# Batch 1's folds begin four units later, w_out's first conversion step moves between P's two parts, and w_in's third transform is cut into three pieces

## The chip, the core and the metric

The kernel runs on one core of a Trainium2 chip. The metric is the time of one execution on the device in microseconds (us); lower is better. The core has TensorE (PE, matrix products; PEld is its loading of weights), VectorE (DVE), ScalarE (ACT) and GpSimd (POOL), each with its own stream of instructions that it works through in order, and SyncE (SP), which here only issues DMA transfers. POOL issues DMA transfers too, and computes between them.

## What is computed

The reference takes a two-dimensional Fourier transform of each of four batches, keeps the real part, and sends the tokens through two feed-forward blocks:

```python
X = np.fft.fft(np.fft.fft(x, axis=1), axis=2).real      # x: 4 x 3072 x 256
h = X @ w_in                                            # 256 -> 2048
g = np.maximum(0.01 * h, h) @ w_out                     # 2048 -> 256
xk = mu_k * g + (1 - mu_k) * g_prev                     # g_prev: the token before
xr = mu_r * g + (1 - mu_r) * g_prev
k = np.maximum(xk @ w_k, 0)
out = 1 / (1 + np.exp(-(xr @ w_r))) * (k * k @ w_v)
```

The weights are float64 in memory.

## The kernel before

**Shape of the work.** The transform over the 256 columns is folded into w_in (in eight pieces of 256 columns, `w_in_mm`), so that h comes out of two half-width products: P (from the even half, tiles `Ph` and `Pl`, a high and a low part) and Q (the odd half, `Qh`, `Ql`). The transform over the 3072 tokens is made of four products a batch, "Pe", "Qe", "Po" and "Qo", each with two tables (`fft_a` and `fft_b`), from a folded copy of the input, `pm`. Each product is taken in high and low parts, three matrix products for one.

**Units.** The first feed-forward block runs in 192 units: four batches b, three tiles ti of 512 token pairs, sixteen blocks u of 128 hidden columns. Inside a batch the unit has the number i = 16 ti + u. A unit (`step`) is, on PE: `mm_b` of this unit (L597, three matmuls), `mm_a` of the next (L585, three), and `outmm` of the unit two before (L608, twelve: `gh` by `uoh`, `gh` by `uol`, `gl` by `uoh`). DVE makes `g` (L674) and the next unit's `ev` (L590), then `gl` (L656); ACT makes the two leaky copies of `g` (L108) and `gh` (L105). `mm_b` needs `ev`, and `outmm` needs `gl` and the piece of w_out that belongs to it.

**Boot.** During batch 0's first tile the weights are still converted from float64, a piece every two units (`boot`). A piece of w_out goes through eight steps: head (ACT, L130), and (DVE, L134), two (DVE, L140), three (DVE, L143), tail (ACT, L148, then POOL, L149), four (ACT, L162, then POOL, L163) and five (DVE, L167, which writes `uol`). Piece q is used by `outmm` of units 2q and 2q + 1.

**Folds.** While batch b runs, batch b + 1's `pm` is made in six folds g (`fold_ops`): `first(g)` has SP load a quarter into `pm` (L210) and two quarters into a buffer `xl` (L211; two buffers in turn); `second(g)` has POOL add the other quarters by accumulating DMA (L215 to L218: the first waits for the load into `pm`, L216 for the load into `xl`, L217 for the addition of L215, and L218 for that of L217); `fin(g)` is a subtraction on DVE (L221) that reads `xl`. There is one `pm`, so that `first(0)` cannot start before the last reader of the old one, Qe's second half at i = 11. The folds' results are first read at i = 36 (Po).

**What sets the order.** Everything is written out by hand: an engine's stream is the order in which the Python code emits instructions, and engines wait for each other by semaphores. For batch 0 the folds are emitted at i = 11 (folds 0 and 1 loaded, fold 0's additions) and then from f0 = 13 to f1 = 36 by the rule `done * (f1 - f0) < 6 * (i - f0 + 1)`, which comes to `fin` at i = 13, 16, 20, 24, 28 and 32; each brings the next `second` and the `first` after that.

**Start.** Ahead of the first unit stand `first_p` and `first_q` (batch 0's Po and Qo, straight into `Ph`, `Pl` and `Q`), then the conversion of w_out's piece 0 (`head0`, `and0`, `two0`, `three0`, `tail0`), and the third piece of `w_in_mm`, half of it after the first `mm_a` and half in `boot(0)`.

Of the kernel before, what the change touches and what calls it, by code (L numbers as in the profile page):

```python
# [78 lines left out]
def fft_mlp_kernel(ctx, tc, xs, x7, x8, x87, tb, tbs, alt, ce, so, mu, w_in, w_out, w_k, w_v, w_r, out):  # L79
    nc = tc.nc  # L80
    ctx.enter_context(tc.manual_schedule())
    V, A, T, G, Q = nc.vector, nc.scalar, nc.tensor, nc.gpsimd, nc.sync
# [21 lines left out]
    def act_copy(o, i):  # L104
        A.activation(o, i, ACTF.Copy)  # L105
# [217 lines left out]
            Q.dma_start(y[0:1, :CW[par]], cd[par][b:b + 1, :CW[par]])  # L323
        classes[b, nm, par] = y

    def first_p(ps, ev):
        fft_mm(0, "Po", 1, ps, True)
        y = pqp.tile([P, CP], F32, tag="P", bufs=2, name="c0Po")
        classes[0, "P", "o"] = y
        hi = mv.tile([P, W], F32R, tag="Ph", bufs=2, name="Ph0_0")  # L330
        lo = mv.tile([P, W], F32R, tag="Pl", bufs=2, name="Pl0_0")
        act_copy(hi[:, :J], ps[:, :J])
        V.scalar_tensor_tensor(y[:, J:2 * J], ev[:, :J], 2.0, ps[:, :J], op0=ALU.mult, op1=ALU.subtract)
        V.tensor_tensor(lo[:, :J], ps[:, :J], hi[:, :J].bitcast(F32), op=ALU.subtract)
        hi_lo(hi[:, J:], lo[:, J:], y[:, J:W])
        return [hi, lo]

    def first_q(ps, ev):
        fft_mm(0, "Qo", 1, ps, True)
        y = pqp.tile([P, CP], F32, tag="Q", bufs=2, name="c0Qo")  # L340
        classes[0, "Q", "o"] = y
        act_copy(y[:, :J], ps[:, :J])
        n = W - J
        V.scalar_tensor_tensor(y[:, J:W], ev[:, :n], -2.0, ps[:, :n], op0=ALU.mult, op1=ALU.add)
        act_copy(y[0:1, :J], cs0[0:1, :J])
        act_copy(y[0:1, J:W], cs0[0:1, J:W])

        def rest():
            V.scalar_tensor_tensor(y[:, W:2 * J], ev[:, n:J], -2.0, ps[:, n:J], op0=ALU.mult, op1=ALU.add)
            act_copy(y[0:1, W:CW["o"]], cs0[0:1, W:CW["o"]])  # L350
        return rest
# [42 lines left out]
            win[q] = f64_parts(win[q], 2, 256, F32R)  # L394


    def w_in_mm(q, halves=(0, 1)):
        if q >= 8:
            return
        if halves[0] == 0:  # L400
            wps[q] = *win[q], ps_s.tile([P, 512], F32, tag="s", name=f"wps{q}")
        fv, r, ps = wps[q]
        win[q] = ps, slice(q * 256, (q + 1) * 256)
        for i in halves:
            tabl, tabr = ((cet, cer), (sot, sor))[i]
            o = ps[:, i * 256:(i + 1) * 256]
            for k in range(2):
                T.matmul(o, tabl[:, k], fv[:, k], start=(k == 0), stop=False)
            for k in range(2):
                T.matmul(o, tabr[:, k], r[:, k], start=False, stop=(k == 1))  # L410

    def w_in_split(q):
        if q >= 8:
            return
        ps, sl = win[q]
        o = ps.rearrange("p (i f) -> p i f", i=2)
        act_copy(wh2[:, :, sl], o)
        V.tensor_tensor(wl2[:, :, sl], o, wh2[:, :, sl].bitcast(F32), op=ALU.subtract)
# [122 lines left out]
    po = fft_a(0, "Po")  # L541
# [1 line left out]
    for g in range(3, 6):  # L543
        fold_odd(g, x0[g])
    w_in_parts(2)
    cur = first_p(*po)
    head0, and0, two0, three0, tail0 = wout[0][3]
    rest_q = first_q(*qo)
    head0()
    and0()  # L550
    rows.release()
    wo = tc.alloc_tile_pool(name="wo", bufs=1)
# [5 lines left out]
    def boot(u):  # L558
        q = u // 2
        if u == 0:  # L560
            w_in_mm(2, (1,))
            three0()
            tail0()
            wout[0][1]()
            w_in_load(4)
        elif u % 2 == 0:
            w_in_row(q + 1)
            w_in_mm(q + 2)
            if q < 8:
                wout[q][0]()  # L570
                wout[q][1]()
            w_in_load(q + 4)
        else:
            w_in_split(q + 2)
            wout[q][2]()
            w_in_parts(q + 3)
            w_out_load(q + 3)
# [243 lines left out]
    rest_q()  # L821
    for b in range(B):

        pe_u, qe_u, f0, f1 = (5, 10, 13, 36) if b == 0 else (1, 4, 10, 36)
        po_u, qo_u = 37, 40
        done = 0
        for ti in range(NT):
# [3 lines left out]
            for u in range(NF):  # L831
                i = ti * NF + u
                x = nx
                if u < NF - 1:
                    nx = unit(b, ti, u + 1, cur, cur_c)
                elif not last:
                    cur, cur_c = nxt, nxt_c
                    nx = unit(nb, nt, 0, cur, cur_c)
                else:
                    nx = None  # L840
                step(x, nx)
                if b == 0 and ti == 0:
                    boot(u)
                if b == 0 and i < 2:
                    next_tab()
                if b == 0 and i == 0:
                    alt2 = work.tile([2, JP], F32, tag="fv", bufs=2, name="alt2")
                    Q.dma_start(alt2, alt)
                if b == 0 and i == 1:
                    even0(0, 1)  # L850
                    even0(1, 1)
                    act_copy(altt[0:2], alt2)
                    V.tensor_tensor(c87[0:1], x87t[:, 0], x87t[:, 1], op=ALU.add)
                if b == 0 and i == 3:
                    chalf = c_a(c8s, "a", True)
                if b == 0 and i == 4:
                    c_b(c8s, "b", "e", *chalf, "yo")

                for kb, kind, k_u in ((b, "Pe", pe_u), (b, "Qe", qe_u), (b + 1, "Po", po_u), (b + 1, "Qo", qo_u)):
                    if kb == B:  # L860
                        continue
                    lag = 2
                    if i in (k_u - 1, k_u + 1):
                        fft_src(kb, kind, (i - k_u + 1) // 2)
                    if i == k_u:
                        half = fft_a(kb, kind)
                    if i == k_u + lag:
                        fft_b(kb, kind, *half)
                    if i in (k_u, k_u + lag):
                        next_tab()  # L870
                if i == qe_u + 1:
                    if b + 1 < B:
                        first, second, fin, _, load7, sum7, fold7 = fold_ops(b + 1)
                        first(0)
                        first(1)
                        load7()
                        second(0)
                if b == B - 1 and i == qe_u + 2:
                    fft.release()
                    w2_alloc()  # L880
                if b + 1 < B:
                    while f0 <= i and done < 6 and done * (f1 - f0) < 6 * (i - f0 + 1):
                        fin(done)
                        if done < 5:
                            second(done + 1)
                        if done < 4:
                            first(done + 2)
                        done += 1
                        if done == 2:
                            sum7()  # L890
                        if done == 4:
                            fold7()
                if i == 13:
                    dc_split(b)
                if 14 <= i < 18:
                    dc_mm(b, i - 14)
                if i == 18:
                    dc_load(b)
                if i == 26:
                    dc_g(b)  # L900
                if b == 0 and i == 34:
                    w2_load[0]()
                if len(w2_steps) > 5 * (len(sources) - n_early):
                    if po_u <= i < po_u + 5 or (b > 0 and i < 5):
                        w2_steps.pop(0)()
                elif b == B - 1 and i > 7 and w2_steps and i % 3:
                    w2_steps.pop(0)()
                if b == B - 1:
                    if i == 33:
                        Q.dma_start(mut, mu)  # L910
                    if i == 36:
                        V.tensor_scalar(omu, mut, -1.0, 1.0, op0=ALU.mult, op1=ALU.add)
                        loaded[0] = load_tile(0)
                    if i == 39:
                        todo = do_prep(0)
                    if i in (40, 42, 44, 46):
                        todo.pop(0)()
                if not last:
                    if u == 8:
                        nxt_c = load_c(nb, nt)  # L920
                    if u == (9 if b or ti else 12):
                        nxt = split_tile(nb, nt, "P")
                    if u == (12 if b or ti else 14):
                        nxt += split_tile(nb, nt, "Q")
# [90 lines left out]
    for ti in range(len(tiles)):  # L1015
# [3 lines left out]
        f0, f1, g0 = (0, 2, 4) if ti else (2, 5, 5)  # L1019
# [3 lines left out]
        for f in range(f0, NK):  # L1023
            ps = ps2.tile([P, 512], F32, tag="k", bufs=2, name="kps")
# [110 lines left out]
```

## Time and profile before

| | |
|---|---|
| median of 3 runs | 1501.49 us (1501.39 to 1501.73) |
| the profiled execution's own time | 1500.71 us |
| its span, first to last instruction | 1498.9 us |
| PE busy | 1475.7 us, 98% |
| DVE busy | 1025.5 us, 68% |
| ACT busy | 893.8 us, 60% |
| POOL busy | 145.4 us, 10% |
| mean granted clock of PE | 0.997 |

The profiled execution took 0.78 us less than the median, and 1.8 us of its time lie outside its span. Shares are of the span. PE's clock has two levels, 1.2 and 2.4 GHz; 1.00 stands for 2.4, and a mean between 0.5 and 1 over a stretch is a mixture in time.

### The profile page before, as it was taken

Reading aid. Unit: us, or ns where it says so; the run is one execution under the profiler, and the core shown is the slowest. Engines: PE = TensorE matmul, PEld = TensorE weight load, DVE = VectorE, ACT = ScalarE, POOL = GpSimd, SP = SyncE. Lnnn points to the kernel's source line nnn. Section 1 sums busy time; section 2 is a strip of 40 time slices with the busy share of each in tenths; the row PEclk is TensorE's granted clock in tenths of the full one; section 3 lists DMA queues with packets and bytes.
Section 4 is the critical chain, followed back from the end, with each engine's and each line's share of the span. In section 5 each row is a group of like instructions: output and inputs, shape, how many; then the busy total and the mean of one; then the engine's idle time right before and its main releaser. Section 6 shows DMA issues by size and latency. Waiting matters only on the chain.

```text
span 1498.9 us, 17784 instructions
## 1 busy us (share of the span) xinstructions
PE 1475.7 (98%) x6520; PEld 1212.7 (81%) x6520; DVE 1025.5 (68%) x1444; ACT 893.8 (60%) x1481; POOL 145.4 (10%) x154
## 2 busy tenths in 40 slices
PE   7997999999999999999999999999999999999998
PEld 4785888888888888888888887888888888888887
DVE  7885667666667666676667765776767676666675
ACT  4674556656556656666566665656555656555554
POOL 2434201122001131010010000000000000000000
PEclk9998999999999999999999999999999999999999
DMA  8755414365123554132320102221212121221200
GB/s 312 200 163 130 71 49 156 102 173 93 29 72 119 192 108 92 39 124 92 109 57 22 56 1 84 84 80 48 85 42 85 45 82 57 71 70 57 71 29 29
DMA packets 86396, 134.24 MB, mean 90 GB/s; under 512 B 29283, under 2 KB 49525, under 8 KB 82724
## 3 DMA queue, kind: packets, MB, share of 16 engines
q1 hardware_dynamic: 70916, 86.49, 17.7%
q0 software_dynamic: 15392, 46.61, 12.4%
q8 instruction: 51, 0.84, 0.2%
q14 instruction: 37, 0.30, 0.1%
HBM read 105.20 MB, written 27.88 MB: 89 GB/s over the span
## 4 chain that ended last, share of the span: by engine, by line
PE 90%; DVE 1%; DMA 1%; POOL 1%; issue 0%; ACT 0%; POOLq 0%; ACTq 0%; DVEq 0%
PE o L608 32%; PE v L975 17%; PE kps L932 17%; PE ps L597 8%; PE ps L585 8%; PE rps L983 4%; DMA pm<-in_xs 1%; PE dps L629 0%; POOL r L163 0%; POOL r L149 0%; PE f1Qe L300 0%; PE f2Qe L300 0%; DMA y<-yo 0%; PE f3Qe L300 0%; PE f3Pe L300 0%
## 5 line engine op out<-in xcount | busy, mean ns | idle before, releaser
L674 DVE SCALAR_TENSOR_TENSOR g<-ev,ps 128x512 f32<-128x512 f32 x192 | 131.7, 686 | 182.3 <-PE ps L597 182.3
L936 ACT ACTIVATE rl<-kps 128x512 f32<-128x512 f32 x190 | 113.5, 597 | 230.7 <-PE kps L932 227.3
L656 DVE TENSOR_TENSOR gl<-g,gh 128x1024 fp32r<-128x1024 f32 x192 | 236.8, 1234 | 1.6 <-ACT gh L105 1.6
L937 DVE SCALAR_TENSOR_TENSOR k<-kps,rl 128x512 f32<-128x512 f32 x190 | 131.3, 691 | 148.6 <-ACT rl L936 147.8
L105 ACT ACTIVATE gh<-g 128x1024 fp32r<-128x1024 f32 x192 | 202.7, 1056 | 49.3 <-PE o L608 47.6
L608 PE MATMUL o<-gh,uol 128*128 128x512 f32 x768 | 213.3, 392 | 9.5 <-DVE uol L167 9.5
L608 PE MATMUL o<-gl,uoh 128*128 128x512 f32 x768 | 212.7, 391 | 0.0
L608 PE MATMUL o<-gh,uoh 128*128 128x512 f32 x768 | 211.3, 389 | 0.0
L108 ACT ACTIVATE g<-ps 128x512 f32<-128x512 f32 x192 | 114.6, 597 | 160.8 <-DVE g L674 159.5
L608 PEld LDWEIGHTS o<-gh,uol 128*128 128x128 f32 x768 | 144.8, 189 | 40.8 <-DVE uol L167 10.9
L608 PEld LDWEIGHTS o<-gl,uoh 128*128 128x128 f32 x768 | 145.3, 189 | 30.4
L608 PEld LDWEIGHTS o<-gh,uoh 128*128 128x128 f32 x768 | 144.2, 188 | 30.5
L590 DVE SCALAR_TENSOR_TENSOR ev<-cb,w,ps 128x512 f32<-128x512 f32 x192 | 143.3, 746 | 2.0
L112 DVE TENSOR_TENSOR k2l<-k,k2h 128x512 fp32r<-128x512 f32 x190 | 129.6, 682 | 0.5 <-ACT k2h L105 0.5
L975 PE MATMUL v<-k2h,wvh 128*128 128x512 f32 x382 | 121.7, 389 | 0.1
L975 PE MATMUL v<-k2l,wvh 128*128 128x512 f32 x382 | 121.5, 389 | 0.0
L975 PE MATMUL v<-k2h,wvl 128*128 128x512 f32 x382 | 121.5, 389 | 0.0
L108 ACT ACTIVATE g<-g 128x512 f32<-128x512 f32 x192 | 120.0, 625 | 0.0
L932 PE MATMUL kps<-mh,wkh 128*128 128x512 f32 x380 | 117.3, 390 | 1.5 <-ACT mh L105 0.8
L105 ACT ACTIVATE k2h<-k 128x512 fp32r<-128x512 f32 x190 | 118.4, 623 | 0.0
L932 PE MATMUL kps<-ml,wkh 128*128 128x512 f32 x380 | 117.2, 390 | 0.1
L932 PE MATMUL kps<-mh,wkl 128*128 128x512 f32 x380 | 117.1, 389 | 0.0
(409 smaller groups left out, 2249.6 us busy)
## 6 DMA issues: line engine op xcount, KB each, us to landing
y<-yo SPq DMA_DIRECT2D x24, 512.0 KB
xa<-y SPq DMA_DIRECT2D x24, 512.0 KB
out_dram<-o SPq DMA_DIRECT2D x23, 512.0 KB
tab_a<-in_tbs POOLq DMA_DIRECT2D x8, 1158.0 KB, 6.2
tab_b<-in_tbs POOLq DMA_DIRECT2D x8, 1158.0 KB, 5.4
tab_c<-in_tbs POOLq DMA_DIRECT2D x6, 1158.0 KB, 5.6
tab_d<-in_tbs POOLq DMA_DIRECT2D x6, 1158.0 KB, 5.8
pm<-in_xs POOLq DMA_DIRECT2D x54, 128.0 KB, 3.2
```

Of the source, the lines that this page charges most:

```text
L105: A.activation(o, i, ACTF.Copy)
L108: A.activation(o, i, ACTF.Prelu, alpha=0.01)
L112: V.tensor_tensor(lo, src, hi.bitcast(F32), op=ALU.subtract)
L585: T.matmul(x["ps"], l[:, f], r, start=(i == 0), stop=(i == 2))
L590: V.scalar_tensor_tensor(x["ev"], x["cb"], w128[:, u:u + 1], x["ps"], op0=ALU.mult, op1=ALU.add)
L597: T.matmul(x["ps"], l[:, f], r, start=False, stop=(i == 2), skip_group_check=True)
L608: T.matmul(po[s][h], w[:, u % HF, h * P:(h + 1) * P], g[:, s], start=(u == 0 and i == 0), stop=(u == NF - 1 and i == 2))
L656: V.tensor_tensor(gl, x["g"], x["gh"].bitcast(F32), op=ALU.subtract)
L674: V.scalar_tensor_tensor(g[:, 1], x["ev"], 2.0, x["ps"], op0=ALU.mult, op1=ALU.subtract)
L932: T.matmul(ps, w[:, k, sl], x[:, k], start=(i == 0), stop=(i == 5))
L937: V.scalar_tensor_tensor(k2, ps, 0.0, r, op0=ALU.max, op1=ALU.mult)
L975: T.matmul(vps[m], w[:, f, m * P:(m + 1) * P], x, start=(f == 0 and i == 0), stop=(f == NK - 1 and i == 2))
```

## The change

Three edits. First, batch 0's loop emits the first loads and additions of batch 1's folds at i = 15 in place of 11 (`l0`), and spreads the rest from f0 = 18 in place of 13, still to f1 = 36: `fin` at i = 18, 21, 24, 27, 30 and 33. For the later batches the numbers are as before. Second, `head0`, the ACT step that begins w_out's piece 0, is called inside `first_p`, between the copies of P's first 384 and last 128 columns, and no longer after `first_q`. Third, `boot(0)` gives out only the first two of the four matmuls of `w_in_mm(2)`'s second half (those that read `fv`), and `boot(1)` gives out the other two (those that read `r`).

```diff
-    def first_p(ps, ev):
+    def first_p(ps, ev, fill):
...
         act_copy(hi[:, :J], ps[:, :J])
+        fill()
         V.scalar_tensor_tensor(y[:, J:2 * J], ev[:, :J], 2.0, ps[:, :J], op0=ALU.mult, op1=ALU.subtract)
...
-    def w_in_mm(q, halves=(0, 1)):
+    def w_in_mm(q, halves=(0, 1), parts=(0, 1)):
...
-            for k in range(2):
-                T.matmul(o, tabl[:, k], fv[:, k], start=(k == 0), stop=False)
-            for k in range(2):
-                T.matmul(o, tabr[:, k], r[:, k], start=False, stop=(k == 1))
+            for k in range(2 if 0 in parts else 0):
+                T.matmul(o, tabl[:, k], fv[:, k], start=(k == 0), stop=False, skip_group_check=True)
+            for k in range(2 if 1 in parts else 0):
+                T.matmul(o, tabr[:, k], r[:, k], start=False, stop=(k == 1), skip_group_check=True)
...
-    cur = first_p(*po)
     head0, and0, two0, three0, tail0 = wout[0][3]
+    cur = first_p(*po, head0)
     rest_q = first_q(*qo)
-    head0()
     and0()
...
         if u == 0:
-            w_in_mm(2, (1,))
+            w_in_mm(2, (1,), (0,))
...
         else:
+            if q == 0:
+                w_in_mm(2, (1,), (1,))
             w_in_split(q + 2)
...
-        pe_u, qe_u, f0, f1 = (5, 10, 13, 36) if b == 0 else (1, 4, 10, 36)
+        pe_u, qe_u, l0, f0, f1 = (5, 10, 15, 18, 36) if b == 0 else (1, 4, 5, 10, 36)
...
-                if i == qe_u + 1:
+                if i == l0:
```

POOL's stream around units 10 to 16. `tab_c` and `tab_d` are tables for batch 1, `r` is the low part of a piece of w_out (the two pairs of L149 and L163 are pieces 6 and 7), `pm` and `xl` are the folds. Before:

```order
L193 DMA tab_c<-in_tbs 128x2316
L215 DMA pm_1001<-in_xs 128x256
L216 DMA xl_0_1002<-in_xs 128x512
L217 DMA pm_1001<-in_xs 128x256
L218 DMA pm_1001<-in_xs 128x256
L149 TENSOR_TENSOR r<-st,h 128x512
L163 TENSOR_TENSOR r<-r,fv 128x512
L193 DMA tab_d<-in_tbs 128x2316
L215 DMA pm_1001<-in_xs 128x256
L216 DMA xl_1_1005<-in_xs 128x512
L217 DMA pm_1001<-in_xs 128x256
L218 DMA pm_1001<-in_xs 128x256
```

With the change the same stretch reads:

```order
L193 DMA tab_c<-in_tbs 128x2316
L149 TENSOR_TENSOR r<-st,h 128x512
L163 TENSOR_TENSOR r<-r,fv 128x512
L193 DMA tab_d<-in_tbs 128x2316
L149 TENSOR_TENSOR r<-st,h 128x512
L163 TENSOR_TENSOR r<-r,fv 128x512
L215 DMA pm_1184<-in_xs 128x256
L216 DMA xl_0_1185<-in_xs 128x512
L217 DMA pm_1184<-in_xs 128x256
L218 DMA pm_1184<-in_xs 128x256
```

Folds 0 and 1, which stood ahead of the additions of pieces 6 and 7, now stand behind both.

ACT's stream at the start, `Ph` and `Qh` being the high parts of P and Q and `h<-st` the step `head0`. Before:

```order
L105 ACTIVATE Ph_0_299<-f0Po 128x384
L105 ACTIVATE Ph_0_299<-c0Po 128x128
L105 ACTIVATE c0Qo<-f0Qo 128x384
L105 ACTIVATE c0Qo<-cs 1x384
L105 ACTIVATE c0Qo<-cs 1x128
L130 ACTIVATE h<-st 128x512
L105 ACTIVATE Qh_0_345<-c0Qo 128x512
```

With the change:

```order
L105 ACTIVATE Ph_0_299<-f0Po 128x384
L130 ACTIVATE h<-st 128x512
L105 ACTIVATE Ph_0_299<-c0Po 128x128
L105 ACTIVATE c0Qo<-f0Qo 128x384
L105 ACTIVATE c0Qo<-cs 1x384
L105 ACTIVATE c0Qo<-cs 1x128
L105 ACTIVATE Qh_0_345<-c0Qo 128x512
```

`h<-st` moved up by four places, from just ahead of `Qh` to just behind the first copy of P.

PE's stream in units 0 and 1, where L597 (L599 with the change) is `mm_b`, L585 (L587) is `mm_a`, and `wps` the third piece of w_in. Before:

```order
L408 MATMUL wps_338<-fv,sot 128x256 x2
L410 MATMUL wps_338<-r,sor 128x256 x2
L597 MATMUL ps<-Qh_0_345,wh_110 128x512
L597 MATMUL ps<-Ql_0_346,wh_110 128x512
L597 MATMUL ps<-Qh_0_345,wl_111 128x512
L585 MATMUL ps<-Ph_0_299,wh_110 128x512
L585 MATMUL ps<-Pl_0_300,wh_110 128x512
L585 MATMUL ps<-Ph_0_299,wl_111 128x512
```

With the change:

```order
L409 MATMUL wps_338<-fv,sot 128x256 x2
L599 MATMUL ps<-Qh_0_345,wh_110 128x512
L599 MATMUL ps<-Ql_0_346,wh_110 128x512
L599 MATMUL ps<-Qh_0_345,wl_111 128x512
L587 MATMUL ps<-Ph_0_299,wh_110 128x512
L587 MATMUL ps<-Pl_0_300,wh_110 128x512
L587 MATMUL ps<-Ph_0_299,wl_111 128x512
L411 MATMUL wps_338<-r,sor 128x256 x2
```

The two matmuls with `r` moved from ahead of unit 1's `mm_b` to behind its `mm_a`. On SP the loads of the folds moved with POOL's additions: behind the first row of the product that unit 14 starts (`dc`), and ahead of the others. DVE's stream changes only in the places of the six `fin`.

## Rows read from the trace of the kernel before

**Rows 1.** PE's waits over the whole run: us in total, times, longest.
```profile
PE o L608 <- DVE uol L167: 9.5, 3, 5.0
```

**Rows 2.** Timeline of PE, units 14 to 17: start, us, what, in brackets idle before.
```profile
110.27 0.50 PE L597 MATMUL ps<-Qh,wh 128*128 128x512 f32 x1
...
117.89 2.08 PE L608 MATMUL o<-gh,uol 128*128 128x512 f32 x4 [5.03 <-DVE uol L167]
...
134.00 2.00 PE L608 MATMUL o<-gh,uol 128*128 128x512 f32 x4 [3.89 <-DVE uol L167]
...
137.98 0.40 PE L597 MATMUL ps<-Qh,wh 128*128 128x512 f32 x1
...
142.57 0.39 PE L597 MATMUL ps<-Qh,wh 128*128 128x512 f32 x1
```

**Rows 3.** Timeline of POOL, 113 to 127 us.
```profile
113.60 0.85 POOL L218 DMA_DIRECT2D pm<-in_xs  x1 [2.40 <-DMA pm<-in_xs]
...
115.85 1.26 POOL L163 TENSOR_TENSOR r<-r,fv 128x512 f32<-128x512 f32 x1
...
126.45 0.86 POOL L217 DMA_DIRECT2D pm<-in_xs  x1 [7.04 <-DMA pm<-in_xs]
```

**Rows 4.** A stretch: length, busy us (count) of PE, PEld, DVE, ACT, POOL; clock, DMA, GB/s.
```profile
118.00:124.00 6.00, 6.00 (x15) 4.29 (x16) 4.66 (x10) 4.33 (x9) 1.41 (x2) 0.51 0.93 258
```

**Rows 5.** Timeline, all engines: w_out's piece 5, ahead of the folds.
```profile
98.43 2.31 POOL L163 TENSOR_TENSOR r<-r,fv 128x512 f32<-128x512 f32 x1
...
100.78 0.69 DVE L167 SCALAR_TENSOR_TENSOR uol<-r,uoh 128x512 fp32r<-128x512 f32 x1 [0.22 <-POOL r L163]
...
102.21 1.07 PE L608 MATMUL o<-gh,uol 128*128 128x512 f32 x4
```

**Rows 6.** Waits for accumulating loads into xl (L216), all 18.
```profile
DMA to landing us min/median/max: 3.7/4.6/9.1
```

**Rows 7.** Timeline: batch 1's fold 0, load and addition; batch 2's last two fins.
```profile
102.35 0.60 SPq L211 DMA_DIRECT2D xl<-in_xs  x1
...
107.62 1.23 POOL L216 DMA_DIRECT2D xl<-in_xs  x1
...
394.22 0.42 DVE L221 TENSOR_TENSOR pm<-xl 128x256 f32<-128x256 f32 x1
...
410.54 0.42 DVE L221 TENSOR_TENSOR pm<-xl 128x256 f32<-128x256 f32 x1
```

**Rows 8.** Timeline, all engines: the first two units.
```profile
26.14 0.31 ACT L105 ACTIVATE Ph<-c0Po 128x128 fp32r<-128x128 f32 x1 [0.73 <-DVE c0Po L333]
...
27.62 0.39 PE L585 MATMUL ps<-Ph,wl 128*128 128x512 f32 x1
...
28.00 0.65 ACT L130 ACTIVATE h<-st 128x512 f32<-128x512 f32 x1
...
28.56 0.61 ACT L105 ACTIVATE Qh<-c0Qo 128x512 fp32r<-128x512 f32 x1
28.69 0.43 DVE L134 TENSOR_SCALAR h<-h 128x512 uint32<-128x512 uint32 x1 [1.03 <-ACT h L130]
29.03 0.74 DVE L590 SCALAR_TENSOR_TENSOR ev<-cb,w,ps 128x512 f32<-128x512 f32 x1
29.69 0.68 DVE L112 TENSOR_TENSOR Ql<-c0Qo,Qh 128x512 fp32r<-128x512 f32 x1
...
30.43 0.50 PE L597 MATMUL ps<-Ql,wh 128*128 128x512 f32 x1
...
31.89 0.75 DVE L590 SCALAR_TENSOR_TENSOR ev<-cb,w,ps 128x512 f32<-128x512 f32 x1
...
32.37 0.59 PE L410 MATMUL wps<-r,sor 128*128 128x256 f32 x2
...
32.80 0.40 PE L597 MATMUL ps<-Qh,wh 128*128 128x512 f32 x1
...
35.20 0.50 PE L597 MATMUL ps<-Qh,wh 128*128 128x512 f32 x1 [0.84 <-DVE ev L590]
```

## Prediction

> **What bounds the kernel now.** PE is busy for 98% of the span, so the first view to read is the list of PE's waits, which says what a change of order can win at all. It is short. The longest entry is `outmm` waiting for `uol`, the low part of a piece of w_out: 9.5 us in three waits [rows 1]. The timeline of PE then shows where these are: one of 5.03 us in unit 14 and one of 3.89 us in unit 16 [rows 2], 8.92 us together; the third is a small one at the start. The next view is the timeline of POOL at the same time, because `uol` waits for an addition on POOL (L163). POOL was not short of work to do; it stood in line. It issued batch 1's folds, and each of their accumulating DMAs waits for the one before: 2.40 us ahead of L218, and then 7.04 us ahead of the next fold's L217 [rows 3]. The additions for w_out's pieces 6 and 7 stand behind these waits in POOL's stream. The last view is the granted clock. After the first wait it was 0.51 from 118 to 124 us, which is the lower of the two levels, 1.2 GHz [rows 4]; and the four matmuls after each wait took 2.08 and 2.00 us, against 1.07 us for such a group of four at the upper level [rows 2, 5]. So each wait is paid for twice, once as idle time and once as slow matmuls.
>
> **The price of the two waits.** `mm_b` of unit 14 starts at 110.27 us and that of unit 17 at 137.98 us: 27.71 us for three units [rows 2]. Unit 17, which has the same work (a full unit and two matmuls for the row `dc`), runs without a wait and takes from 137.98 to 142.57 us, 4.59 us [rows 2]. Three such units are 13.77 us. What is lost is 27.71 - 13.77 = 13.94 us: 8.92 us idle, and 5.0 us because the clock was down.
>
> **First edit, the later folds.** It removes no instruction. The additions of pieces 6 and 7 now have nothing ahead of them on POOL that waits for a fold. Do they then come in time? Piece 5 answers this, for it went through the same steps with no fold ahead: its `uol` started at 100.78 us and took 0.69, so it was ready at 101.47 us, and PE reached the matmuls that read it at 102.21 us without a wait: 0.74 us to spare [rows 5]. That was with L163 at 2.31 us, beside a busy DVE; behind the waits, beside an idle DVE, the same addition took 1.26 us [rows 3, 5]. I take the long one for pieces 6 and 7, as DVE will be busy there too.
>
> The Trainium skill has a rule for this difference ("SBUF — State Buffer", section "Who interferes with whom"): a VectorE instruction with two operands in SBUF and a GpSimd instruction that reads SBUF exclude each other, and the later one waits until the other is done. The two durations of L163 agree with it. By the rule the additions of pieces 6 and 7 are slower once DVE no longer stalls; by the rows they go from 1.26 to 2.31 us, 1.05 us each, which is the state that piece 5 was in.
>
> So the forecast is that both waits go, and the slow clock behind them. I take 13.6 of the 13.94 us: 0.3 us are left for unit 16, where Q's split for the next tile, piece 7's conversion and the `dc` row meet on DVE and ACT, now in full-speed units of 4.59 us. The upper bound is 13.94. The lower bound is what is left if the same additions come late by a few us each; it is a rival below.
>
> What covers the folds in their new place? The first loads of fold 0 go out at i = 15 and its `fin` stands at i = 18: three units, 3 x 4.59 = 13.8 us. Before, its load into `xl` was issued at 102.35 us and POOL's addition at 107.62 us, 5.3 us later [rows 7]; such an addition lands after 4.6 us in the median and 9.1 us at most [rows 6]: 9.9 us, or 14.4 at worst, with DVE some way into its unit by then. From fold 2 on a `xl` buffer has from `fin(g)` to `fin(g + 2)`, six units. A plain unit is 4.08 us (the last two `fin` of a batch, four units apart, stand 16.32 us apart [rows 7]), so six are 24.5 us, against the same 14.4 us at worst. The DMAs themselves cost nothing new: they are the same ones, and what they could delay now, POOL's next work, is a table for i = 37. On SP the loads are moved behind the first `dc` row, and `xl`'s third load, which has to wait for `fin(0)`, no longer has three `dc` rows behind it. Without that cover, each us that a `fin` is late holds DVE, and after about a unit PE: one us for one.
>
> **Second edit, head0 earlier.** At the start the first `mm_b` waits for DVE, and DVE waits for ACT. DVE stood 1.03 us for `h` (L134), because `h` (28.00 us, 0.65 us long) came behind Q's copies; only then did it make `ev` (29.03 us) and `Ql` (29.69 us), for which PE's second matmul of `mm_b` waited until 30.43 us [rows 8]. In its new place `h` costs nothing, because ACT stood idle there for 0.73 us, waiting for P's last 128 columns [rows 8]; if that gap were not there, `Ph` and with it the first `mm_a` would come 0.65 us later. With `h` out of the way `Qh` can start at 28.00 us in place of 28.56 and is ready at 28.61 us. `ev` can start when `mm_a` ends, 27.62 + 0.39 = 28.01 us, so at about 28.04 us; `Ql` follows 0.66 us behind it as before (29.69 - 29.03), at 28.70 us, ready at 29.38 us; and PE's second matmul, which stood 0.06 us behind the end of `Ql` (30.43 against 29.69 + 0.68), starts at 29.44 us in place of 30.43 us [rows 8]: 0.99 us. The chain that follows, from `g` over the tail of piece 0 to its `uol`, hangs on this and moves with it. The bounds are 0 (some other wait takes the place) and 1.03 us; I take 1.0.
>
> **Third edit, the three pieces.** Unit 1's `mm_b` stood behind the two matmuls with `r`, which took 32.80 - 32.37 = 0.43 us of PE, and unit 2's `mm_b` then waited 0.84 us for `ev` [rows 8]. Moved into that wait the two matmuls are free. But PE wins little by reaching unit 1's `mm_b` earlier: its `ev` starts at 31.89 us and takes 0.75 us, until 32.64 us, and `mm_b` started at 32.80 us [rows 8]. So it can come forward by about 0.1 us and no more. Bounds: 0, and 0.43 us if `ev` too came forward. I take 0.1.
>
> **The sum.** 13.6 + 1.0 + 0.1 = 14.7 us. The profiled execution took 1500.71 us, so the same execution would take 1486.0 us; the median of the runs shown is 0.78 us above that execution, and 1501.49 - 14.7 = 1486.8 us is the forecast.
>
> **The rivals.**
> *The waits shrink, but stay.* For it: 0.74 us to spare is little [rows 5], pieces 6 and 7 meet other work on DVE than piece 5 did, and after an idle stretch of several us the clock was down for as long again [rows 2, 4]. Against it: all eight pieces go through the same steps, and of PE's three waits for them the two long ones belong to the two pieces that had folds ahead [rows 1, 2]. Price: a wait of 1 to 3 us in each of the two units, at the upper clock or with part of the slow matmuls: 2 to 7 us given back, so 1488.8 to 1493.8 us.
> *The rule of the shared port, taken further.* The two durations of L163 differ by 1.05 us [rows 3, 5], and for pieces 6 and 7 a second delay of that size could fall on DVE's own instructions ahead of `uol`. Then each `uol` comes 1.05 - 0.74 = 0.3 us too late for PE [rows 5], 0.6 us for both, so 1487.4 us. The rule that would make it so is the one named above from the Trainium skill; no row here shows it on DVE.
> *The folds become late (slower than before).* The folds have 18 units in place of 23, and they share the DMA engines with batch 0's results. If a `fin` waits, DVE stands, with everything behind it. To eat 14.7 us and another 3 us, the six `fin` must wait 3 us each on average; for folds 2 to 5 that takes a round of 24.5 + 3 = 27.5 us where 14.4 us is the worst that the rows give [rows 6, 7]. Time: from 1504.5 us.
> *The change does not do what it says.* Another wait of equal length could stand behind the folds, as a late load of the last pieces, which the waits on POOL now hide. Nothing in the waits of PE or POOL speaks for it; the start would still give 1.1 us: about 1500 us.
>
> **How the numbers follow.** Forecast (both waits gone): 0.74, with a range of its own from 1486.1 (all terms at their upper bounds, 13.94 + 1.03 + 0.43 = 15.4 us) to 1488.3. The shared port taken further: 0.05. Waits that shrink but stay: 0.15. No change to speak of: 0.04. Late folds: 0.02. The 8 in 10 range reaches from 1485.5, which is that best case less a few tenths between runs and in the reading of the rows, into the case of waits that stay, to 1491.0. A measurement of this kernel can tell about 0.2%, 3 us, from no change. The first three cases are faster by more than that: 0.94. The fourth is the same: 0.04. The last is slower: 0.02.
>
> **What would show it.** In the profile after, PE's waits for `uol` should be down from 9.5 us to under 1 us, with no stretch of the granted clock under 0.9 between 100 and 150 us, and unit 14 to unit 17 in about 13.8 us. POOL should issue L163 twice in that stretch at about 2.3 us, with no DMA of a fold between. At the start `ev` should begin at about 28.0 us and DVE have no wait for `h`; unit 2's wait for `ev` should be about half of 0.84 us. All `fin` should start without a wait for a DMA, as those of [rows 7] did. Wrong would be: a wait of DVE for `xl` in units 18 to 33, a new wait of PE in unit 14 or 16, or a wait of ACT for a `dc` row, whose DMA now follows four loads of folds on SP.

## The result, and the profile of the changed kernel

The changed kernel took 1489.45 us (median of 6 runs, 1489.06 to 1489.79), the kernel before 1501.61 us (median of 6, 1501.09 to 1503.11). The ratio is 0.9917, 95% interval 0.9904 to 0.993. The profiled execution took 1489.41 us, 11.30 us less than that of before, with a span of 1487.6 us and a mean granted clock of 0.999. The forecast was 1486.8 us: faster, as said, but 2.65 us short of it.

PE's waits of the changed kernel (us in total, times, longest), to be set against [rows 1]:

```profile
PE wps L409 <- DVE fv L140: 6.4, 1, 6.4
PE ps L599 <- DVE ev L592: 2.4, 2, 1.8
...
PE o L610 <- DVE uol L167: 0.5, 1, 0.5
```

Both long waits for `uol` are gone; what is left of that row is the small one at the start. But the wait of `mm_b` for `ev` now has an entry of 1.8 us. The timeline, all engines, of units 13 to 18 (start, us, what, in brackets idle before) shows where that one is and what made it:

```profile
106.51 1.30 POOL L149 TENSOR_TENSOR r<-st,h 128x512 f32<-128x512 f32 x1 [5.99 <-issue]
...
106.99 1.25 DVE L322 SCALAR_TENSOR_TENSOR c0Qe<-fe0Qe,c0Qe 128x384 f32<-128x384 f32 x1 [0.62 <-ACT c0Qe L105]
...
107.89 1.49 POOL L163 TENSOR_TENSOR r<-r,fv 128x512 f32<-128x512 f32 x1
...
108.15 1.51 DVE L112 TENSOR_TENSOR Pl<-c0Po,Ph 128x256 fp32r<-128x256 f32 x1
...
109.58 0.41 DVE L112 TENSOR_TENSOR Pl<-c0Pe,Ph 128x256 fp32r<-128x256 f32 x1
...
110.52 0.73 DVE L592 SCALAR_TENSOR_TENSOR ev<-cb,w,ps 128x512 f32<-128x512 f32 x1
...
111.31 0.50 PE L599 MATMUL ps<-Qh,wh 128*128 128x512 f32 x1 [1.79 <-DVE ev L592]
...
114.53 1.85 PE L610 MATMUL o<-gh,uol 128*128 128x512 f32 x4
...
117.18 1.30 POOL L149 TENSOR_TENSOR r<-st,h 128x512 f32<-128x512 f32 x1 [7.28 <-issue]
...
118.56 1.29 POOL L163 TENSOR_TENSOR r<-r,fv 128x512 f32<-128x512 f32 x1
...
118.72 1.41 DVE L112 TENSOR_TENSOR Ql<-c0Qo,Qh 128x256 fp32r<-128x256 f32 x1 [1.69 <-ACT Qh L105]
...
122.19 0.41 PE L599 MATMUL ps<-Qh,wh 128*128 128x512 f32 x1
...
126.75 0.39 PE L599 MATMUL ps<-Qh,wh 128*128 128x512 f32 x1
...
131.33 0.39 PE L599 MATMUL ps<-Qh,wh 128*128 128x512 f32 x1
```

Read POOL and DVE together. No DMA of a fold stands between POOL's pairs. (L149 is a multiplication in the code and L163 an addition; the two together are called additions here.) L149 ends at 106.51 + 1.30 = 107.81 us, and DVE's L322, which was begun meanwhile, ends 0.43 us later; L163 ends at 109.38 us, and `Pl` 0.28 us later. DVE's timeline of the kernel before has the same three instructions without an addition on POOL beside them (what POOL did there was to issue fold 0's DMAs, L215 at 107.07 us and L216 at 107.62 us):

```profile
107.72 0.56 DVE L322 SCALAR_TENSOR_TENSOR c0Qe<-fe0Qe,c0Qe 128x384 f32<-128x384 f32 x1 [0.62 <-ACT c0Qe L105]
108.20 0.42 DVE L112 TENSOR_TENSOR Pl<-c0Po,Ph 128x256 fp32r<-128x256 f32 x1
108.54 0.42 DVE L112 TENSOR_TENSOR Pl<-c0Pe,Ph 128x256 fp32r<-128x256 f32 x1
```

L322 grew by 0.69 and the first `Pl` by 1.09 us: 1.78 us. `ev` stands behind both, and PE waited 1.79 us for it. The windows of the changed kernel (length, busy us and count of PE, PEld, DVE, ACT, POOL; clock, DMA, GB/s), beside [rows 4], add the second half of the price:

```profile
113.00:116.00 3.00, 3.00 (x9) 2.32 (x8) 2.97 (x6) 2.27 (x4) 0.00 (x0) 0.50 0.33 123
116.00:119.00 3.00, 3.00 (x15) 2.19 (x14) 1.28 (x3) 1.84 (x5) 1.74 (x2) 0.97 0.01 3
```

The granted clock was 0.50, the lower level, for some 3 us after the wait, and the four matmuls at 114.53 us took 1.85 us. From the `mm_b` at 111.31 to that of unit 17 at 126.75 us are 15.44 us, against 27.71 before [rows 2]; three units at 4.58 us, the pace of unit 17 here (126.75 to 131.33 us), are 13.74, so 1.70 us went into the stretch of slow clock. With the wait ahead of it, 3.49 us were lost again. This is the profiled execution. Of the six runs two had a mean granted clock of 0.999 (1489.41 and 1489.48 us) and four of 1.000 (1489.06 to 1489.79 us). Since 3 us at half clock take 0.001 off the mean of 1488 us, the clock of those four was down for about half as long at most, by this estimate; and yet they took the same time. So the 1.70 us would not all come back with the clock; the first edit alone, below, shows what takes their place.

The start, timeline of all engines, to be set against [rows 8]:

```profile
26.19 0.31 ACT L105 ACTIVATE Ph<-c0Po 128x128 fp32r<-128x128 f32 x1 [0.15 <-DVE c0Po L334]
...
28.11 0.75 DVE L592 SCALAR_TENSOR_TENSOR ev<-cb,w,ps 128x512 f32<-128x512 f32 x1
...
28.84 0.69 DVE L112 TENSOR_TENSOR Ql<-c0Qo,Qh 128x512 fp32r<-128x512 f32 x1
...
29.59 0.50 PE L599 MATMUL ps<-Ql,wh 128*128 128x512 f32 x1
...
31.85 0.50 PE L599 MATMUL ps<-Qh,wh 128*128 128x512 f32 x1
...
34.35 0.50 PE L599 MATMUL ps<-Qh,wh 128*128 128x512 f32 x1 [0.61 <-DVE ev L592]
```

The second matmul of `mm_b` came 0.84 us earlier (29.59 against 30.43) and unit 2's `mm_b` 0.85 us (34.35 against 35.20). Unit 17's came 126.75 against 137.98: 11.23 us, all of the 11.30 us up to a tenth.

### The profile page after: what moved, and what is told of

The parts are those of the page before. It is cut to its first block, busy times and chain, and to the rows that moved or that the text cites. A ratio compares the mean times of both kernels' runs of the same rounds, so it can differ in the third digit from the quotient of the medians.

```text
span 1487.6 us, 17785 instructions
## 1 busy us (share of the span) xinstructions
PE 1472.1 (99%) x6520; PEld 1210.7 (81%) x6520; DVE 1028.2 (69%) x1444; ACT 894.1 (60%) x1481; POOL 145.7 (10%) x154
## 4 chain that ended last, share of the span: by engine, by line
PE 93%; DVE 4%; ACT 1%; POOL 1%; DMA 0%; issue 0%; ACTq 0%; POOLq 0%; DVEq 0%
PE o L610 34%; PE v L977 17%; PE kps L934 17%; PE ps L599 8%; PE ps L587 8%; PE rps L985 4%; PE dps L631 1%; POOL r L163 0%; DVE fv L140 0%; DVE gl L658 0%; PE wps L409 0%; DVE g L676 0%; POOL r L149 0%; DMA st<-in_w_in 0%; DVE x L261 0%
## 5 line engine op out<-in xcount | busy, mean ns | idle before, releaser
L658 DVE TENSOR_TENSOR gl<-g,gh 128x1024 fp32r<-128x1024 f32 x192 | 236.9, 1234 | 1.6 <-ACT gh L105 1.6
```

The source lines that it names most:

```text
L658: V.tensor_tensor(gl, x["g"], x["gh"].bitcast(F32), op=ALU.subtract)
```

## The experiments

The theory: the gain comes from POOL's line, which no longer stands ahead of w_out's pieces 6 and 7; and what is missing comes from POOL's additions, which hold DVE's instructions beside them. The rivals: the gain has another source, or DVE is simply overloaded in these units, or the issuing of DMAs on POOL is what slows it.

### The first edit alone

On the kernel before:

```diff
-        pe_u, qe_u, f0, f1 = (5, 10, 13, 36) if b == 0 else (1, 4, 10, 36)
+        pe_u, qe_u, l0, f0, f1 = (5, 10, 15, 18, 36) if b == 0 else (1, 4, 5, 10, 36)
-                if i == qe_u + 1:
+                if i == l0:
```

> The first edit alone on the kernel before. If POOL's line (w_out's pieces 6 and 7 behind batch 1's folds) is what the change removed, this gives all of the gain but the 0.8 us of the start: about 1490.3 us, PE's waits for uol down to the one of 0.5 us at the start, and the new wait of unit 14's mm_b for ev as in the changed kernel (1.8 us). If instead the earlier start of the first units mattered for what happens at 110 us, the gain is clearly smaller, 1493 us or more, and a wait for uol stays.

Measured: 1490.39 us (1490.14 to 1490.72), ratio 0.992 (0.9905 to 0.9935), span 1488.3 us. So this edit carries nearly all of the gain. Its timeline of PE has two waits in units 14 to 16; the last row is unit 17:

```profile
112.32 0.50 PE L597 MATMUL ps<-Qh,wh 128*128 128x512 f32 x1 [1.77 <-DVE ev L590]
...
122.79 0.47 PE L597 MATMUL ps<-Qh,wh 128*128 128x512 f32 x1 [1.05 <-DVE ev L590]
...
127.42 0.39 PE L597 MATMUL ps<-Qh,wh 128*128 128x512 f32 x1
```

and its window over unit 14 reads

```profile
110.00:115.00 5.00, 3.23 (x15) 2.35 (x14) 5.00 (x9) 2.52 (x5) 0.91 (x2) 1.00 0.69 232
```

The wait in unit 14 is the same as in the whole change (1.77 and 1.79 us), but here the clock stayed at the upper level. A second wait, in unit 16, stands where the whole change has none; there `Ql` took 0.72 and 1.50 us beside piece 7's additions. Unit 14 to unit 17 took 127.42 - 112.32 = 15.10 us, 1.33 over the 13.77 of three full-speed units; with the wait ahead, 3.10 us were lost without any slow clock, against 3.49 with it.

### The other two edits, each alone

The two edits as the diff of the change has them, each on the kernel before.

> The second edit alone. Expected: ev of unit 0 starts at about 28.1 us in place of 29.03, the second matmul of the first mm_b about 0.85 us earlier, and the waits of 5.0 and 3.9 us for uol stay: 0.8 us less, about 1500.7 us. Rival: the step hides behind some other wait of the start and nothing moves by unit 2.

> The third edit alone. Expected: unit 1's mm_b starts 0.1 us earlier at most and now waits for ev; unit 2's wait for ev falls from 0.84 to about 0.5 us, because the two matmuls fill it; unit 2's mm_b itself starts within 0.1 us of 35.20: no change that a time can show. Rival: ev was not what bounded unit 1, and the edit gives up to 0.43 us.

With the second edit alone the one run took 1499.72 us, with the third alone 1502.07 us, beside 1502.63 us (median of 7) for before; single runs can't settle a microsecond, so the traces decide. PE's timelines of unit 2, second edit alone and then third alone:

```profile
34.46 0.50 PE L597 MATMUL ps<-Qh,wh 128*128 128x512 f32 x1 [0.84 <-DVE ev L590]
```

```profile
35.48 0.50 PE L599 MATMUL ps<-Qh,wh 128*128 128x512 f32 x1 [0.61 <-DVE ev L592]
```

The second edit brings unit 2 forward by 0.74 us (35.20 before [rows 8]); its wait of 0.84 us stays. The third cuts that wait to 0.61 us and brings nothing: unit 2 came 0.28 us later than before in a run whose second matmul of `mm_b` had already been 0.28 us later (30.71 against 30.43). The waits for `uol` stay in both (9.4 and 9.9 us in total).

### Folds in the old place, pieces 6 and 7 on DVE

The other way out of POOL's line: the kernel before, with L149 and L163 of these two pieces on DVE.

```diff
-            G.tensor_tensor(z["r"], z["r"], z["f"], op=ALU.add)
+            z.get("e", G).tensor_tensor(z["r"], z["r"], z["f"], op=ALU.add)
...
-            wout[q] = f64_hi_lo(..., *((mv, "gl") if q < 1 else (stage, "f")))
+            wout[q] = f64_hi_lo(..., *((mv, "gl") if q < 1 else (stage, "f")), V if q >= 6 else G)
```

> The folds stay where they were before, but the two additions of w_out's pieces 6 and 7 run on DVE and not on POOL, so that they no longer stand in POOL's line. If the line is the cause, PE's waits of 5.03 and 3.89 us for uol go although no fold has moved, at the price of 1.4 us more on DVE in each of the two units, of which up to 1 us may show as a wait for ev: 1488 to 1491 us. If the folds' transfers themselves are the cause (they slow a load or the DMA queues at that time), the waits stay and the time is 1500 us or more.

Measured: 1489.59 us (1488.69 to 1490.07), ratio 0.9914 (0.9897 to 0.993). The long waits for `uol` go as well (0.5 us left), with the folds where they were: it is POOL's line that held them, and not the folds' loads or their place. Timeline, POOL and DVE:

```profile
108.62 1.23 POOL L216 DMA_DIRECT2D xl<-in_xs  x1
...
108.74 0.56 DVE L322 SCALAR_TENSOR_TENSOR c0Qe<-fe0Qe,c0Qe 128x384 f32<-128x384 f32 x1
```

L322 took 0.56 and `Pl`, just behind it, 0.42 us each while POOL issued this DMA: issuing did not hold DVE here. PE waits for `ev` 0.80 us in unit 14 and 1.56 us in unit 16. The first comes from DVE's new work, instructions of 0.69 us; ahead of the second DVE had also stood 0.94 us before the `fin` at 113.90 us, waiting for fold 0's DMA, and worked without a wait from there to unit 16's `ev`.

### The changed kernel again

> The changed kernel once more, as the measure for the other runs on the same chip: about 12 us under the kernel before. Its profile also tells whether the slow clock behind unit 14's wait of 1.8 us is always there or not.

Measured: 1489.47 us (1489.28 to 1489.79), ratio 0.9916 (0.9901 to 0.9931). The same picture: a wait of 1.77 us in unit 14, L322 1.26 us, `Pl` 1.51 us, and a clock of 0.79 from 110 to 115 us. As to whether the slow clock is always there, the four runs' mean clocks suggest that it is not, or not as long: 0.999 in two (the profiled one among them) and 1.000 in the other two, with times no shorter (1489.28 and 1489.59 against 1489.36 and 1489.79 us).

### Fold 0 back at i = 11, the others late

The edit puts back what is emitted at `l0`: the loads and additions of fold 0 and, on SP, the load of fold 1.

```diff
-        pe_u, qe_u, l0, f0, f1 = (5, 10, 15, 18, 36) if b == 0 else (1, 4, 5, 10, 36)
+        pe_u, qe_u, l0, f0, f1 = (5, 10, 11, 18, 36) if b == 0 else (1, 4, 5, 10, 36)
```

> The changed kernel with fold 0's loads and additions put back to i = 11, ahead of piece 6 on POOL; the other folds stay from i = 18 on. If the line on POOL is the cause, unit by unit, exactly the first wait for uol comes back (about 5 us in unit 14, and slow matmuls behind it), the one in unit 16 does not, and the wait for ev in unit 14 goes, because POOL adds while DVE stands: about 1493 us. If the folds' transfers disturb in general, both waits come back in part.

Measured: 1494.51 us (1494.45 to 1495.01), ratio 0.9949 (0.9933 to 0.9966). Timeline, POOL and PE of unit 14:

```profile
114.32 0.85 POOL L218 DMA_DIRECT2D pm<-in_xs  x1 [3.33 <-DMA pm<-in_xs]
...
116.56 1.26 POOL L163 TENSOR_TENSOR r<-r,fv 128x512 f32<-128x512 f32 x1
...
118.61 2.07 PE L610 MATMUL o<-gh,uol 128*128 128x512 f32 x4 [6.35 <-DVE uol L167]
```

One fold's additions ahead of one piece give back one wait for `uol`, and unit 16 has none. The wait is 6.35 us, where about 5 were expected, and the time 1.5 us above the expected 1493. Piece 6's additions come late here, while DVE stands, and L322 took 0.56 and `Pl` 0.42 us: without the neighbour there is no holding. `Ql`, which met piece 7's L163 at 124.13 us, took 1.50 us.

### P's split one unit later

`split_tile` makes P's `Ph` and `Pl` for the next tile; in batch 0's first tile it is moved from behind unit 12 to behind unit 13, out of the way of piece 6's additions.

```diff
-                    if u == (9 if b or ti else 12):
+                    if u == (9 if b or ti else 13):
```

> The changed kernel, with P's split for the second tile at unit 13 in place of 12, behind ev of unit 14 on DVE. If POOL's additions for piece 6 hold DVE's instructions with two operands in SBUF, only c0Qe (1.25 us in place of 0.56) is still held ahead of ev, g and ev themselves read one operand from PSUM and keep 0.68 and 0.74 us, and unit 14's wait of 1.8 us falls to 0.3 or less; the low clock behind it goes too. Q's split in unit 14 then meets piece 7's additions and may cost 0.7 us in unit 16: about 1486.6 us. If it is the mere number of instructions on DVE in unit 12, moving 0.84 us of work leaves about 1 us of the wait: 1488 us or more.

Measured: 1488.19 us (1488.12 to 1488.38), ratio 0.9907 (0.9893 to 0.9922). The wait in unit 14 is gone, `Pl` took 0.41 us twice and the clock stayed at 1.00. But a wait has come up in unit 16. Timeline, POOL, DVE and PE:

```profile
117.12 0.72 DVE L112 TENSOR_TENSOR Ql<-c0Qo,Qh 128x256 fp32r<-128x256 f32 x1 [1.02 <-ACT Qh L105]
...
117.63 1.35 POOL L163 TENSOR_TENSOR r<-r,fv 128x512 f32<-128x512 f32 x1
...
117.76 1.51 DVE L112 TENSOR_TENSOR Ql<-c0Qe,Qh 128x256 fp32r<-128x256 f32 x1
...
120.86 0.47 PE L599 MATMUL ps<-Qh,wh 128*128 128x512 f32 x1 [1.71 <-DVE ev L592]
```

The collision is the same, one piece later: units 14 and 15 now run on time, and so Q's split meets piece 7's additions head on. The time alone lies in the rival's range (1488 us or more); what speaks against the rival is the trace, for it wanted about 1 us of unit 14's wait to stay, and none did.

### Q's split ahead of the row dc in unit 14

As above, with Q's split called earlier in unit 14, ahead of the `dc` row:

```diff
+                if b == 0 and i == 14:
+                    nxt += split_tile(nb, nt, "Q")
...
-                    if u == (12 if b or ti else 14):
+                    if (b or ti) and u == 12:
                         nxt += split_tile(nb, nt, "Q")
```

> As p_split_13, and Q's split in unit 14 stands ahead of the dc row and no longer behind it, so that ACT's Qh does not wait for PE's dc product, and DVE's Ql come before piece 7's additions on POOL have begun. By the theory of held instructions Ql takes 0.42 us twice in place of 1.41 + 0.41, and unit 16 has no wait for ev: about 1486 us, 0.5 us under p_split_13. By the rival nothing changes against p_split_13.

Measured: 1488.28 us (1488.1 to 1488.55), ratio 0.9908 (0.9893 to 0.9923): no gain. `Ql` began 0.53 us earlier, at 116.59 us, but POOL's L149 had begun at 116.19, and `Ql` took 1.19 and 1.51 us. The step that was to keep the two apart did not, so this run does not tell the theory from its rival.

### Both splits at unit 13

```diff
-                    if u == (9 if b or ti else 12):
+                    if u == (9 if b or ti else 13):
                         nxt = split_tile(nb, nt, "P")
-                    if u == (12 if b or ti else 14):
+                    if u == (12 if b or ti else 13):
                         nxt += split_tile(nb, nt, "Q")
```

> P's and Q's splits for the next tile both stand at unit 13, ahead of POOL's additions for piece 7 (116.2 us and later). Theory that POOL's additions hold DVE where they meet: Ql takes 0.42 us twice, no wait of PE in units 14 and 16, about 1486.5 us (1488.2 of the version with only P's split there, less its wait of 1.71 us). Rival, that DVE's and ACT's load in these units is the cause, wherever the split stands: the wait moves to unit 14 or 15 with 1 to 2 us, 1488 us or more.

Measured: 1486.41 us (1486.24 to 1486.7), ratio 0.9894 (0.9878 to 0.9911): the fastest of all, about 3 us better than the change. Timeline, POOL, DVE and PE:

```profile
108.28 1.50 POOL L163 TENSOR_TENSOR r<-r,fv 128x512 f32<-128x512 f32 x1
...
109.93 0.50 PE L599 MATMUL ps<-Qh,wh 128*128 128x512 f32 x1
...
111.94 0.41 DVE L112 TENSOR_TENSOR Pl<-c0Pe,Ph 128x256 fp32r<-128x256 f32 x1
112.28 0.41 DVE L112 TENSOR_TENSOR Ql<-c0Qo,Qh 128x256 fp32r<-128x256 f32 x1
112.61 0.41 DVE L112 TENSOR_TENSOR Ql<-c0Qe,Qh 128x256 fp32r<-128x256 f32 x1
...
117.13 1.31 POOL L149 TENSOR_TENSOR r<-st,h 128x512 f32<-128x512 f32 x1 [6.82 <-issue]
...
123.98 0.39 PE L599 MATMUL ps<-Qh,wh 128*128 128x512 f32 x1
```

Over units 12 to 14 DVE does the same work as before the move, but all of the splits between POOL's pairs (until 109.78 and from 117.13 us), and PE has no wait in units 14 to 16. Two instructions are still held, L322 (1.26 us) and later `gl` (2.25 us), and PE waits for neither. That speaks against a DVE that is simply overloaded. Units 14 to 16 take 123.98 - 109.93 = 14.05 us.

### One piece's additions on DVE

With the switch of engines shown above, once for piece 7 on the version with P's split at unit 13 (`V if q == 7 else G`), once for piece 6 on the changed kernel (`V if q == 6 else G`).

> P's split at unit 13, Q's where it was, and the two additions of piece 7 on DVE in place of POOL (0.69 us each, more work for DVE). Theory that POOL's additions hold DVE: Ql takes 0.42 us twice, which saves 1.4 us, and DVE spends the same 1.4 us on the additions, so that PE's wait in unit 16 stays at about 1.5 us: 1488.0 to 1488.4 us. Rival, that Ql is slow for a reason of its own: Ql stays at 1.2 us or more and the wait grows to about 3 us, 1489.5 us.

> The changed kernel with the two additions of piece 6 on DVE in place of POOL (0.69 us each). Theory that POOL's additions hold DVE: the dc row's instruction falls from 1.25 to 0.56 us and Pl from 1.51 to 0.42, 1.78 us, against 1.38 us of new work ahead of ev, so PE's wait in unit 14 falls from 1.79 us to about 1.3 or less; 1487.5 to 1489.0 us, by whether the clock falls behind it. Rival, that these instructions are slow for another reason: they stay, and the wait grows to 3 us, 1491 us.

Measured: 1487.15 us (1487.04 to 1487.19), ratio 0.9899 (0.9885 to 0.9914), for piece 7, and 1488.39 us (1488.27 to 1488.73), ratio 0.9908 (0.9893 to 0.9923), for piece 6. The timeline of the latter, DVE and PE:

```profile
106.61 0.69 DVE L149 TENSOR_TENSOR r<-st,h 128x512 f32<-128x512 f32 x1
107.33 0.69 DVE L163 TENSOR_TENSOR r<-r,fv 128x512 f32<-128x512 f32 x1
107.94 0.55 DVE L322 SCALAR_TENSOR_TENSOR c0Qe<-fe0Qe,c0Qe 128x384 f32<-128x384 f32 x1
108.41 0.42 DVE L112 TENSOR_TENSOR Pl<-c0Po,Ph 128x256 fp32r<-128x256 f32 x1
...
110.47 0.50 PE L599 MATMUL ps<-Qh,wh 128*128 128x512 f32 x1 [0.79 <-DVE ev L592]
```

With more work on DVE and less beside it, DVE is done earlier. L322 and `Pl` are back at 0.55 and 0.42 us. The waits shrink more than worked out beforehand (0.79 us in unit 14, where 1.3 or less was expected; 0.75 us in unit 16 for piece 7, where 1.5 were expected), probably because the additions partly fill time in which DVE stood for ACT anyway: 0.62 us ahead of L322 in the change, 1.02 us ahead of `Ql` in the version with P's split at unit 13. With piece 6 on DVE piece 7 stays on POOL: `Ql` took 0.71 and 1.50 us beside it, and unit 16 waited 1.05 us at a clock of 1.00.

## Why the prediction was right in the main, and where not

**The first edit: mechanism right, size off.** Shown by the edit alone and from the other side by pieces 6 and 7 on DVE and by fold 0 put back: the waits for `uol` came from the additions' place behind the folds on POOL, and they went. The term of 13.6 us measured 11.23 at unit 17, less the 0.81 us that the start already brought (`outmm` of unit 11 at 106.63 against 107.44 us): 10.4. The step that failed is "0.3 us are left for unit 16, where Q's split for the next tile, piece 7's conversion and the `dc` row meet on DVE and ACT". DVE met POOL's additions ahead of unit 14 as well, with the `c0Qe` step (L322) and P's split, and the price in the profiled execution was 3.49 us: 1.79 idle and 1.70 of slow clock; 13.94 - 3.49 = 10.45. Unit 16 had no wait in the change, though `Ql` took 1.41 us there. It did wait in each of the four profiled runs in which `Ql` was held and the clock stayed at 1.00: 1.05 us in the first edit alone and with piece 6 on DVE, 1.71 and 1.73 us in the first two versions with P's split at unit 13. So it was probably the slow matmuls that gave DVE the time, and the 0.3 us were too little for unit 16 too. Where the collision is taken away (both splits at unit 13), the term is 27.71 - 14.05 = 13.66 us, which is what was forecast.

**The long durations of L163.** "I take the long one for pieces 6 and 7" was wrong: L163 took 1.49 and 1.29 us, not 2.31. POOL came first this time, and DVE was the one that waited. The rival "the shared port, taken further" had the mechanism, at a chance of 0.05 (1487.4 us), but put it ahead of `uol`, where 0.74 us of slack would have left 0.6 us in all. It fell on the instructions ahead of `ev`, where one unit's PE hangs on it directly and the clock followed. The time measured lies in the span of the other rival, waits that shrink but stay, though not by its mechanism: no wait for `uol` stayed. The forecast's own case, both waits gone, ended at 1488.3 us; that the time lies within the stated 1485.5 to 1491.0 us it owes to the room left for a case that did not happen, and to that extent it was luck.

The Trainium skill ("SBUF — State Buffer", "Who interferes with whom") has the rule in full: "Issue order, not op shape, decides who blocks", and a VectorE instruction with at most one input in SBUF, outside what the page calls the 2-port perf modes, does not contend. Both agree with the runs. L163 was the longer in [rows 5], L322, `Pl` and `Ql` were here; and `g` and `ev`, which read `ps` in PSUM, took 0.68 and 0.74 us beside an L163 (108.33 and 108.93 us, P's split at unit 13).

The prediction states the rule for both directions, but its sum used it for the delay of POOL alone, that of L163 in [rows 5], which started at 98.43 us while DVE's `gl` ran (98.37 us, 1.22 us long). Its "no row here shows it on DVE" holds for the rows that it gives, but not for the trace of the kernel before, which has the other direction too. The timeline, POOL and DVE, before the folds:

```profile
90.87 1.50 POOL L149 TENSOR_TENSOR r<-st,h 128x512 fp32r<-128x512 f32 x1 [2.38 <-issue]
...
91.79 0.99 DVE L112 TENSOR_TENSOR sl0Qe<-t0Qe,sh0Qe 128x384 fp32r<-128x384 f32 x1 [0.59 <-ACT sh0Qe L105]
...
102.53 0.56 DVE L112 TENSOR_TENSOR sl0Qe<-t0Qe,sh0Qe 128x384 fp32r<-128x384 f32 x1 [0.59 <-ACT sh0Qe L105]
```

Begun while POOL's L149 ran, the same instruction took 0.99 us, without it 0.56. The question to put was which instructions of DVE with two inputs in SBUF stand where the additions will be; around 108 us there were three, L322 and the two `Pl`, and the first two were held, by 0.69 and 1.09 us.

**The second edit.** Forecast 1.0 us; `ev` began at 28.11 us (forecast 28.0), DVE's wait of 1.03 us for `h` is gone, and the second matmul came 0.84 us earlier in the change, unit 2 0.74 us earlier with the edit alone. Right, 0.2 us too high.

**The third edit.** Forecast 0.1 us, measured 0 alone, and 0.85 - 0.74 = 0.1 us beside the second. Unit 2's wait fell to 0.61 us, not to half of 0.84.

**The folds.** All 18 `fin` started without a wait for a DMA and took 0.42 us each. The cover worked out at 13.8 us for fold 0 held.

**The signs.** Wrong were "no stretch of the granted clock under 0.9", "unit 14 to unit 17 in about 13.8 us" and the durations of L163; the new wait of PE in unit 14 was among the things named that would make the prediction wrong.

## What to carry to other kernels

When an engine is freed from a line, its work moves in time: look at what stands beside it in the new place, not only at whether it comes in time. In these runs an addition on POOL and a DVE instruction with both inputs in SBUF that met cost the later one the rest of the earlier one, so put the movable block (here the splits) into the gap between POOL's pairs. Removing one wait also moved the next meeting; after each repair the next unit must be read again.

## What the runs showed of the hardware

- A wait of nearly the same length cost clock in one execution and not in another: after 1.79 us in unit 14 of the change (1.77 when it ran again) the granted clock fell to 0.50; after 1.77 us in unit 14 of the first edit alone and 1.71 us in unit 16 with P's split at unit 13 it stayed at 1.00. It is not a matter of the kernel alone: among the runs of the change, and of the first edit alone, some have a mean clock of 0.999 and some of 1.000. What makes the difference stays open.
- Being held can cost nothing. With both splits at unit 13, DVE's `gl` (L658) took 2.25 us beside the L163 at 118.52 us, against 1.21 or 1.22 without one, and PE did not wait for it.
